# Gated linear attention and a capacity-routed mixture of experts: the low parts of the weights by accumulating DMAs, the middle layer's residuals on GpSimd, and routing operands in other places

## The chip, the cores and the metric

The kernel runs on one core of a Trainium2 chip. The core has a matmul engine (TensorE, PE in the profile), a vector engine (VectorE, DVE), a scalar engine (ScalarE, ACT), GpSimd (POOL), a queue that issues transfers (SyncE, SP), and 16 DMA engines. SBUF is the working memory of 128 partitions; PSUM holds what TensorE writes. The metric is the device time of one execution in microseconds; lower is better.

## The reference

The first part is a linear attention with a decay for each channel, 4 batches of 8 heads, 768 steps, 48 channels. Its output is read as 3072 tokens of 384 values. The second part gives every token to one of 8 experts: the scores are taken in falling order over all tokens and experts, and a token goes to the first expert on its list that has room for it. Each expert takes exactly 384 tokens and applies two layers, 384 to 1024 to 384.

```python
state = alpha[:, :, t, :, None] * state + np.einsum('bhd,bhe->bhde', k[:, :, t], v[:, :, t])
y[:, :, t] = np.einsum('bhd,bhde->bhe', q[:, :, t], state)
...
logits = x @ w_gate
order = np.argsort(-logits.flatten())
for idx in order:
    tok, e = int(idx) // E, int(idx) % E
    if assigned[tok] >= 0 or counts[e] >= cap:
        continue
    assigned[tok] = e
    counts[e] += 1
for e in range(E):
    mask = assigned == e
    h = np.maximum(x[mask] @ w1[e], 0.0)
    out[mask] = h @ w2[e]
```

## The kernel before

The attention stage takes the first 142 us or so. It writes the tokens' rows to a scratch array in HBM (`x_dram`) and leaves the scores of all tokens in SBUF (`L`).

Then two jobs run beside each other to the end.

**Routing.** Experts are filled one after the other, in the order in which they become full. A search (`search`) finds the score at which the next expert has its 384 tokens: the scores' bits are taken as five digits (`BITS`), and for each digit VectorE compares all keys with all values of the digit (`cmp`, L653), TensorE counts by expert with 24 small matmuls (L683), and VectorE decides (`g`, L686), TensorE sums (L690), VectorE takes the digit (`k`, L692) and takes it off the keys (`nd`, L695). At the end of a search some twenty short VectorE instructions find which expert was filled (`es`, `ei`), which tokens it got, and each token's rank in it (`cum`, `rts`, `offs`, `v`). `update` then moves the remaining tokens to their next choice and makes new keys. `extract` turns ranks into row numbers (`idx`, L828), and GpSimd gathers the expert's rows from `x_dram` with three indirect DMAs (`xr`, L833). Many of the small routing operands lie in one PSUM bank (`zb`, "z" in the profile), which the attention no longer needs.

**Experts.** As soon as an expert's number is known, SP loads its weights in two halves, `w1r` and `w2r`, 768 KB each (`weights`). Each matmul operand is used as a rounded high part and a low part, the rest, and each product is taken as high x high, high x low and low x high. `split` makes the parts of the weights: ScalarE copies the high parts `w1h` (L876) and `w2h` (L894). The low part of w2 is made by a ScalarE copy with the sign turned (`w2l`, L892) to which a DMA issued by GpSimd adds the raw weights (L896). The low part of w1 is made by GpSimd, `w1l = w1r - w1h` (L884), in four pieces per half; from the seventh block on each of these pieces waits for the relu of an earlier block (`GATE`, `paced`). `prep` turns the gathered rows with TensorE (L909), copies the high part with ScalarE (`xh`, L914) and subtracts with VectorE (`xl`, L916).

The hidden layer is worked in 8 blocks of 128 units. For a block, `ffn1` does nine matmuls of 128x128 by 128x384 (L930); ScalarE applies the relu (`hf`, L937) and copies the high part (`hh`, L939), VectorE subtracts for the low part (`hl`, L940). `ffn2`, which comes two blocks later, does nine matmuls (L956) into three banks that collect the output over all eight blocks. At an expert's end ScalarE copies the output (`yo`, L961) and GpSimd scatters the rows (L966). PSUM has two banks for the blocks of `ffn1`.

The order in which each engine issues its work is fixed when the kernel is built. `Plan` holds every operation with an engine, an estimated cost, what it reads and writes, and a rank, and simulates the engines: whichever engine can start next takes the operation of the highest rank that is ready. The rank is a base plus the length of the chain behind the operation. The base of routing is 2000 (`CHAIN`), of the extraction 1900 (`SIDE`), and of expert work 1000 less 32 per expert and 3.6 per block (`at`). Each engine then works through its list in order and waits where its next instruction waits. `lat` is the plan's time from a transfer's issue to its landing.

The first expert's second halves of the weights wait until its three gathers have landed (`rows0` and the manual dependency in `weights`).

Of the kernel before, what the change touches and what calls it, by code (L numbers as in the profile page):

```python
# [164 lines left out]
def gla_moe_kernel(ctx, tc, q, k, v, alpha, w_gate, w1, w2, out):  # L165
# [419 lines left out]
    for z in range(2):
        t = {}
        for name, shape, dtype in (
# [3 lines left out]
                ("sg", [NU], I32), ("un", [NU], F32), ("o", [NU, E], BF), ("d0", [NU], BF), ("vi", [NU], I32),  # L591
# [2 lines left out]
        t["nd"] = [rw.tile([128, NU], BF, name=f"nd{z}{j}") for j in range(nb - 1)]
# [68 lines left out]
    def search(i):
# [7 lines left out]
        dh = [("d0", z)] if i else []  # L671
        for t, bits in enumerate(BITS):
# [20 lines left out]
            if not final:  # L693
                nd = s["nd"][t]
                v_(0.24, lambda d=d, nd=nd, t=t: nc.vector.scalar_tensor_tensor(  # L695
                    nd, d, s["k"], dig[:, t + 1], op0=OP.subtract, op1=OP.add),
                   r=H("k") + dh + ["dig"], w=[("nd", z, t)])
# [14 lines left out]
        v_(0.2, lambda: nc.vector.tensor_scalar(s["cl"], ramp, es, None, op0=OP.is_equal), r=H("es"), w=H("cl"))  # L712
# [8 lines left out]
        v_(0.16, lambda: nc.vector.tensor_copy(s["rts"], s["cum"][:, :, NU - 1]), r=[("cum", z, 0), ("cum", z, 1)],  # L721
# [325 lines left out]
```

## Time and profile before

| | |
|---|---|
| median of 3 runs | 479.87 us (474.65 to 480.53) |
| the profiled execution | 480.41 us, span of its instructions 478.7 us |
| attention stage | 0 to about 142 us |
| first matmul of an expert | 179.8 us |
| last row numbers known (`idx`) | 406.6 us |
| last output copied | 469.3 us |

A group's row in the profile names line, engine, operation, output and inputs, the shapes and the count; then the busy time in us, the mean of one in ns, and the idle time of that engine just before these instructions with what ended it. In the list of waits each row names the waiting engine and line, then the one it waited for, the total in us, the number of times and the longest. A row of the timeline begins with the start and the length in us. "Granted clock" is the share of TensorE's full clock that it was given.

### The profile page before, as it was taken

Reading aid. Unit: us, or ns where it says so; the run is one execution under the profiler, and the core shown is the slowest. Engines: PE = TensorE matmul, PEld = TensorE weight load, DVE = VectorE, ACT = ScalarE, POOL = GpSimd, SP = SyncE. Lnnn points to the kernel's source line nnn. Section 1 sums busy time; section 2 is a strip of 40 time slices with the busy share of each in tenths; the row PEclk is TensorE's granted clock in tenths of the full one; section 3 lists DMA queues with packets and bytes.
Section 4 is the critical chain, followed back from the end, with each engine's and each line's share of the span. In section 5 each row is a group of like instructions: output and inputs, shape, how many; then the busy total and the mean of one; then the engine's idle time right before and its main releaser. Section 6 shows DMA issues by size and latency. Waiting matters only on the chain.

```text
span 478.7 us, 11002 instructions
## 1 busy us (share of the span) xinstructions
PE 426.7 (89%) x4326; PEld 379.3 (79%) x4326; DVE 301.6 (63%) x823; ACT 225.2 (47%) x415; POOL 229.2 (48%) x257
## 2 busy tenths in 40 slices
PE   4999999899999778899598889998879989999992
PEld 1788988788887657798498778887769989999991
DVE  6878787978736944955757686775865775222210
ACT  1356555465430035457227447346328557675431
POOL 6767867577500061339126525444228357663402
PEclk9599999999999988799979989999979999999998
DMA  8848987550110057476284484475375199643101
GB/s 295 313 164 276 336 276 224 178 184 18 68 54 16 7 181 195 92 272 149 51 283 98 115 276 105 99 250 148 67 274 151 51 305 370 155 115 67 49 1 51
DMA packets 37684, 76.33 MB, mean 159 GB/s; under 512 B 3584, under 2 KB 17920, under 8 KB 37632
## 3 DMA queue, kind: packets, MB, share of 16 engines
q1 hardware_dynamic: 32256, 53.60, 33.3%
q0 software_dynamic: 5376, 22.02, 19.1%
q8 instruction: 34, 0.56, 0.5%
q14 instruction: 18, 0.15, 0.1%
HBM read 53.59 MB, written 9.44 MB: 132 GB/s over the span
## 4 chain that ended last, share of the span: by engine, by line
PE 64%; DVE 21%; issue 7%; POOL 2%; DMA 2%; ACT 2%; SPq 0%; POOLq 0%; DVEq 0%; ACTq 0%
PE s L930 16%; PE y L956 5%; PE lg L956 5%; PE st L683 5%; PE s L402 5%; PE xt L956 5%; PE xt L390 4%; DVE cmp L653 4%; PE y L453 4%; PE y L446 4%; PE lg L465 2%; DVE te L362 2%; PE s L912 2%; PE st L414 2%; PE xt L909 1%
## 5 line engine op out<-in xcount | busy, mean ns | idle before, releaser
L884 POOL TENSOR_TENSOR w1l<-w1r,w1h 128x384 fp32r<-128x384 f32 x64 | 68.2, 1106 | 57.4 <-ACT hf L937 44.6
L937 ACT ACTIVATE hf<-s 128x384 f32<-128x384 f32 x64 | 31.3, 490 | 101.9 <-PE s L930 73.5
L940 DVE TENSOR_TENSOR hl<-hf,hh 128x384 fp32r<-128x384 f32 x64 | 42.3, 665 | 47.1 <-ACT hh L939 46.9
L833 POOL DMA_INDIRECT xr<-x_dram,idx x24 | 28.5, 1186 | 90.8 <-DVE idx L828 79.7
L930 PE MATMUL s<-xl,w1h 128*128 128x384 f32 x192 | 48.0, 359 | 9.6 <-ACT hf L937 6.4
L930 PE MATMUL s<-xh,w1l 128*128 128x384 f32 x192 | 45.9, 347 | 1.9 <-ACT hf L937 1.9
L966 POOL DMA_INDIRECT out_dram<-yo,idx x24 | 26.9, 1119 | 43.0 <-ACT yo L961 39.4
L930 PE MATMUL s<-xh,w1h 128*128 128x384 f32 x192 | 46.3, 352 | 0.6 <-ACT xh L914 0.6
L930 PEld LDWEIGHTS s<-xl,w1h 128*128 128x128 f32 x192 | 34.2, 196 | 13.5 <-ACT hf L937 9.9
L653 DVE TENSOR_TENSOR cmp<-nd,iota 128x1536 bf16<-128x1536 bf16 (+4 forms) x32 | 41.6, 1310 | 0.8
L876 ACT ACTIVATE w1h<-w1r 128x768 fp32r<-128x768 f32 x32 | 26.0, 834 | 29.6 <-DMA w1r<-in_moe_w_dram 29.6
L683 PEld LDWEIGHTS <-cmp 128*128 128x128 bf16 x816 | 30.4, 118 | 12.1 <-DVE cmp L653 6.9
L372 POOL TENSOR_TENSOR kh<-rk,te 128x512 f32<-128x512 f32 (+1 forms) x24 | 29.4, 1227 | 18.6 <-DVE te L362 14.6
L683 PE MATMUL st<-o,cmp 128*128 128x8 bf16 x816 | 33.1, 175 | 4.8 <-DVE cmp L653 3.8
L402 PE MATMUL s<-qh,kh 64*128 64x128 f32 x384 | 31.6, 301 | 6.2 <-DVE qh L372 5.8
L930 PEld LDWEIGHTS s<-xh,w1l 128*128 128x128 f32 x192 | 34.5, 193 | 2.6 <-issue 1.6
L939 ACT ACTIVATE hh<-hf 128x384 fp32r<-128x384 f32 x64 | 33.6, 526 | 5.6 <-PE y L956 2.6
L405 POOL TENSOR_SCALAR_AFFINE_SELECT sm<-sm 128x1024 f32<-128x1024 f32 x24 | 26.8, 1115 | 18.7 <-ACT sm L404 17.1
L930 PEld LDWEIGHTS s<-xh,w1h 128*128 128x128 f32 x192 | 34.6, 195 | 1.0 <-ACT xh L914 1.0
L402 PEld LDWEIGHTS s<-qh,kh 64*128 64x128 f32 x384 | 25.4, 198 | 11.6 <-DVE qh L372 6.7
L372 POOL TENSOR_TENSOR qh<-rq,tp 128x512 f32<-128x512 f32 (+1 forms) x24 | 29.4, 1227 | 5.2 <-DVE tp L368 4.1
L362 DVE TENSOR_TENSOR_SCAN te<-al,z 128x511 f32<-128x511 f32 (+2 forms) x26 | 30.9, 1189 | 0.9
(193 smaller groups left out, 1019.8 us busy)
## 6 DMA issues: line engine op xcount, KB each, us to landing
w1r<-in_moe_w_dram SPq DMA_DIRECT2D x16, 768.0 KB, 6.1
w2r<-in_moe_w_dram SPq DMA_DIRECT2D x16, 768.0 KB, 8.0
w2l<-w2r POOLq DMA_DIRECT2D x16, 768.0 KB, 6.4
al<-in_alpha_dram SPq DMA_DIRECT2D x24, 260.0 KB, 4.3
rk<-in_k_dram SPq DMA_DIRECT2D x24, 256.0 KB, 4.6
rq<-in_q_dram SPq DMA_DIRECT2D x24, 256.0 KB, 4.1
rv<-in_v_dram SPq DMA_DIRECT2D x24, 192.0 KB, 4.1
x_dram<-xg SPq DMA_DIRECT2D x6, 768.0 KB, 5.3
```

The source lines that it names most:

```text
L362: nc.vector.tensor_tensor_scan(te.t[:, lo:top][:, ::-1], al.t[:, lo + 1:top + 1][:, ::-1], zb[:, lo + 1:top + 1][:, ::-1], al.t[:, 4 * C + ...
L372: eng.tensor_tensor(out_.t[:, us].rearrange("p u c -> p (u c)"), x.t[:, lo:hi], f.t[:, lo:hi], op=OP.mult)
L402: nc.tensor.matmul(sc.t[:, h, u], kh.t[hs, u], qh.t[hs, u], start=True, stop=True)
L653: v_(0.12 + 0.00054 * nt * (js.stop - js.start), lambda js=js: nc.vector.tensor_tensor(words(dst, nt, js), keyed(d, nt, js), each(iotas[t] ...
L683: nc.tensor.matmul(rt[:, 32:40], dst[:, j // U, :, j % U], o[:, j], start=(j == 0), stop=(j == NU - 1))
L833: last_gather[0] = nc.gpsimd.indirect_dma_start(out=xr.t[:, b], out_offset=None, in_=x_dram, in_offset=bass.IndirectOffsetOnAxis(ap=idxs[i ...
L884: x = nc.gpsimd.tensor_sub(l1.t[:, :, c2], r1.t[:, :, c2], h1.t[:, :, c2])
L930: nc.tensor.matmul(o.t.rearrange("p a b -> p (a b)")[:, :CAP], a.t[:, d, cs_], x.t[:, d], start=(n == 0 and d == 0), stop=(n == 2 and d == ...
L937: paced[FB * i + q] = nc.scalar.activation(hf.t, src(), AF.Relu)
L939: add(A_, 0.47, lambda: nc.scalar.activation(hh.t, hf.t, AF.Copy), r=[hf], w=[hh])
L940: v_(0.5, lambda: nc.vector.tensor_sub(hl.t, hf.t, hh.t), r=[hf, hh], w=[hl], port=True)
L956: nc.tensor.matmul(flat(y.t)[:, :Dm], a.t[:, bs], x.t[:, j], start=(q == 0 and n == 0), stop=(q == FB - 1 and n == 2))
```

## The change

- **Low parts of w1.** ScalarE writes `-w1r`, rounded, into `w1l`, in two pieces per half, and a DMA issued by GpSimd adds `w1r` to the whole half, as was done for w2 before. GpSimd's 64 subtractions and their waits for relus (`GATE`, `paced`) are gone. `ffn1`'s third product of each block now needs the sum of the whole half.
- **Residuals of the middle layer.** `hl = hf - hh` moves from VectorE to GpSimd, at a base of 3000, above all other work. VectorE's `xl` also gets a base of 3000.
- **Routing operands.** `rts` is summed by one reduction over `ms` and `qe`, which now lie side by side in PSUM, instead of copied from the ends of the two scans. `ramp` and `pcs` get copies in the PSUM bank for the uses in the chain (`cl`, `oh`). The scaled digits (`dig1`) move from the PSUM bank to SBUF, and the keys (`d0`, `nd`) alternate between two tiles.
- **First expert.** Its second halves of the weights no longer wait for the gathers.
- **The plan's figures.** Landing times of 7.0 us for loads (6.0 before) and 8.5 us for sums (6.0), 0.52 us for `hh`, and 0.035 us between two VectorE operations that follow each other in the PSUM bank (`OWN`).

The diff, without the plan's new bookkeeping of the bank:

```diff
-GATE = 6
-GATHER, LOAD = 3.2, 6.0
+OWN = {"asg", "pen", "dig", "chu", "qe", "m", "ch", "val", "ms", "v1", "ramp"}
+HL_BASE, XL_BASE = 3000.0, 3000.0
+GATHER, LOAD, SUM = 3.2, 7.0, 8.5
...
-    pchu, asg, pm, pch, pqe, pms, pv1 = (mine(120 + NU * j, NU) for j in range(7))
+    pchu, asg, pm, pch, pms, pqe, pv1 = (mine(120 + NU * j, NU) for j in range(7))
+    both = mine(120 + NU * 4, 2 * NU).rearrange("p (a j) -> p a j", j=NU)
...
+    pramp, ppc = mine(296 + NU * E, E), mine(296 + NU * E + E, 1)
+    keys = [rw.tile([128, NU], BF, name=f"key{j}") for j in range(2)]
+    dig1 = rw.tile([128, nb, NU], F32, name="dig1")
...
-                nd = s["nd"][t]
+                nd, kt = keys[(t + 1) % 2], "key%d" % ((t + 1) % 2)
...
-        v_(0.2, lambda: nc.vector.tensor_scalar(s["cl"], ramp, es, None, op0=OP.is_equal), r=H("es"), w=H("cl"))
+        v_(0.2, lambda: nc.vector.tensor_scalar(s["cl"], pramp, es, None, op0=OP.is_equal), r=H("es") + ["ramp"], w=H("cl"))
...
+        def totals():
+            with nc.allow_low_precision(reason="counts up to 24"):
+                nc.vector.tensor_reduce(s["rts"], both, axis=X, op=OP.add)
+        v_(0.2, totals, r=["ms", "qe"], w=H("rts"))
...
-        v_(0.16, lambda: nc.vector.tensor_copy(s["rts"], s["cum"][:, :, NU - 1]), r=[("cum", z, 0), ("cum", z, 1)],
-           w=H("rts"))
...
-            v_(0.28, lambda: nc.vector.scalar_tensor_tensor(pdig, pdi, 1.0, scale, op0=OP.add, op1=OP.mult), w=["dig"])
+            v_(0.28, lambda: nc.vector.scalar_tensor_tensor(dig1, pdi, 1.0, scale, op0=OP.add, op1=OP.mult),
+               r=["dig"], w=["dig1"])
...
-            if i == 0 and hf:
-                tc.add_manual_dep(x.ins, last_gather[0].ins.name, ...
-        wait = ["rows0"] if i == 0 and hf else []
...
+            add(A_, 0.84, lambda c=c: nc.scalar.activation(l1.t[:, :, c], r1.t[:, :, c], AF.Copy, scale=-1.0),
+                r=[r1], w=[(l1, a)])
             add(A_, 0.84, lambda c=c: nc.scalar.activation(h1.t[:, :, c], r1.t[:, :, c], AF.Copy),
                 r=[r1], w=[(h1, a)])
-            for b in range(2):
...
-                    x = nc.gpsimd.tensor_sub(l1.t[:, :, c2], r1.t[:, :, c2], h1.t[:, :, c2])
...
+            if a:
+                add(G_, 1.0, lambda: nc.gpsimd.dma_start(l1.t.bitcast(F32), r1.t, accum_op=OP.add, max_dma_last_dim=8192),
+                    r=[r1, (l1, 0), (l1, 1)], w=[(l1, "sum")], lat=SUM)
...
+            pl.base = XL_BASE
             v_(0.55, lambda x=x, bs=bs: nc.vector.tensor_sub(xl.t[:, :, bs], x.t[:, :DB], xh.t[:, :, bs]),
...
-        for n, (a, x, ra, rx) in enumerate(((h1, xh, (h1, j // 2), xh), (h1, xl, (h1, j // 2), xl), (l1, xh, (l1, j), xh))):
+        for n, (a, x, ra, rx) in enumerate(((h1, xh, (h1, j // 2), xh), (h1, xl, (h1, j // 2), xl), (l1, xh, (l1, "sum"), xh))):
...
-        add(A_, 0.47, lambda: nc.scalar.activation(hh.t, hf.t, AF.Copy), r=[hf], w=[hh])
-        v_(0.5, lambda: nc.vector.tensor_sub(hl.t, hf.t, hh.t), r=[hf, hh], w=[hl], port=True)
+        add(A_, 0.52, lambda: nc.scalar.activation(hh.t, hf.t, AF.Copy), r=[hf], w=[hh])
+        pl.base = HL_BASE
+        add(G_, 1.1, lambda: nc.gpsimd.tensor_sub(hl.t, hf.t, hh.t), r=[hf, hh], w=[hl], port=True)
```

More of the change, by code (lines that the diff above doesn't have):

```diff
@@ L39, in __init__ @@
     def __init__(self):
-        self.ops, self.writer, self.readers, self.base, self.spin = [], {}, {}, 0.0, None
+        self.ops, self.writer, self.readers, self.base, self.spin, self.own = [], {}, {}, 0.0, None, set()
     def buf(self, kind):
@@ L64, in add @@
         before.discard(n)
+        if OWN.intersection(x for x in (*r, *w) if isinstance(x, str)):
+            self.own.add(n)
         self.ops.append((eng, cost, fn, sorted(before), HOP[eng] if lat is None else lat, port, bufs, self.base, mode))
@@ L91, in order @@
         open_ = {i for i in range(n) if not missing[i]}
-        done, ends, last = [], {}, {}
+        done, ends, last, bank = [], {}, {}, {}
         def since(kind, u, eng):
@@ L100, in order @@
                 eng, _, _, _, _, shared, bufs, _, _ = ops[i]
-                t = max(ready[i], free.get(eng, 0.0), port if shared else 0.0)
+                t = max(ready[i], free.get(eng, 0.0), port if shared else 0.0, bank.get(eng, 0.0) if i in self.own else 0.0)
                 for b in bufs:
@@ L116, in order @@
             free[eng] = end - OVER.get(eng, 0.0)
+            bank[eng] = end + SELF.get(eng, 0.0) if i in self.own else 0.0
             if shared:
@@ L590, in gla_moe_kernel @@
                 ("lw", [NU, E], F32), ("offs", [2], F32), ("v", [NU], F32), ("oh", [1], F32), ("sel", [NU], F32),
[L591 removed]
+                ("sg", [NU], I32), ("un", [NU], F32), ("o", [NU, E], BF), ("vi", [NU], I32),
                 ("wi", [NU], I32), ("wb", [NU], BF), ("bk", [NU, NB], F16), ("rhs", [NU, NB], F16), ):
             t[name] = rw.tile([128] + shape, dtype, name=f"{name}{z}")
[L594 removed]
         sets.append(t)
@@ L775, in update @@
         v_(0.35, lambda: nc.vector.tensor_tensor(n["o"], ramp_b, row(chu, E), op=OP.is_equal), r=["chu"], w=[("o", zn)])
-        st.update(chu=chu, o=n["o"], dig=pdig, d=n["d0"], cmp=parts if more else None)
+        st.update(chu=chu, o=n["o"], dig=dig1, d=keys[0], cmp=parts if more else None)
     def search_last(i):
@@ L832, in fetch @@
             def fetch(b=b):
-                last_gather[0] = nc.gpsimd.indirect_dma_start(
+                nc.gpsimd.indirect_dma_start(
                     out=xr.t[:, b], out_offset=None, in_=x_dram,
                     in_offset=bass.IndirectOffsetOnAxis(ap=idxs[i % 4][:, b:b + 1], axis=0))
-            add(G_, 1.2, fetch, r=[("idx", i % 4)] + ([("xd", g) for g in range(NG)] if i == 0 else []), w=[(xr, b)] + (["rows0"] if i == 0 and b == NB - 1 else []), lat=GATHER)
+            add(G_, 1.2, fetch, r=[("idx", i % 4)] + ([("xd", g) for g in range(NG)] if i == 0 else []), w=[(xr, b)], lat=GATHER)
         return xr
@@ L855, in load_w @@
             if which:
-                x = nc.sync.dma_start(r2.t, w2v[bass.ds(ev, 1), :, qs].rearrange("e p c d -> p (e c) d"))
+                nc.sync.dma_start(r2.t, w2v[bass.ds(ev, 1), :, qs].rearrange("e p c d -> p (e c) d"))
             else:
-                x = nc.sync.dma_start(r1.t, w1v[bass.ds(ev, 1), :, :, fs].rearrange("e p c f -> p (e c) f"))
-            if i == 0 and hf:
-                tc.add_manual_dep(x.ins, last_gather[0].ins.name,
-                                  mybir.DependencyInfo(mybir.DependencyClass.Sync, mybir.DependencyReason.DATA),
-                                  reason="rows of the first expert before its later weights")
-        wait = ["rows0"] if i == 0 and hf else []
+                nc.sync.dma_start(r1.t, w1v[bass.ds(ev, 1), :, :, fs].rearrange("e p c f -> p (e c) f"))
         for which, b in ((0, r1), (1, r2)):
-            add("SP", 2.4, lambda which=which: load_w(which), r=[("ei", i % 2)] + wait, w=[b], lat=LOAD)
+            add("SP", 2.4, lambda which=which: load_w(which), r=[("ei", i % 2)], w=[b], lat=LOAD)
         return r1, r2
```

37 lines of the change are left out of this document (12 added, 25 removed).

## The prediction

> **What bounds the kernel now.** I read the page first, then the stretches of 20 us, the groups of TensorE, its waits, and at last the timeline around the longest wait.
>
> ```profile
> span 478.7 us, 11002 instructions
> PE 426.7 (89%) x4326; PEld 379.3 (79%) x4326; DVE 301.6 (63%) x823; ACT 225.2 (47%) x415; POOL 229.2 (48%) x257
> ...
> PE 64%; DVE 21%; issue 7%; POOL 2%; DMA 2%; ACT 2%; SPq 0%; POOLq 0%; DVEq 0%; ACTq 0%
> ```
>
> The chain that ends last is TensorE first, VectorE second; ScalarE, GpSimd and the DMAs hold 2% each. The change touches nothing before 142 us but two small copies, so the expert stage is the one to read. It begins and ends here (timelines of PE and of ACT):
>
> ```profile
> 179.81 2.29 PE L930 MATMUL s<-xh,w1h 128*128 128x384 f32 x6 [0.58 <-ACT xh L914]
> ```
>
> ```profile
> 468.29 0.49 ACT L961 ACTIVATE yo<-y 128x384 f32<-128x384 f32 x1 [2.59 <-PE y L956]
> ```
>
> That is 288.5 us. What must TensorE do in it? The stretches give the pace where nothing disturbs it, and the granted clock where something does (columns: stretch, length, busy us and instructions of PE, PEld, DVE, ACT, POOL, then granted clock, DMA share, GB/s):
>
> ```profile
> 180.00:200.00 20.00, 16.82 (x117) 14.89 (x118) 13.01 (x47) 9.69 (x16) 5.81 (x6) 0.84 0.58 149
> 200.00:220.00 20.00, 20.00 (x183) 18.91 (x183) 12.10 (x28) 11.20 (x19) 8.74 (x8) 0.89 0.73 218
> 240.00:260.00 20.00, 18.74 (x188) 17.36 (x187) 13.78 (x24) 10.22 (x17) 9.31 (x9) 0.87 0.73 225
> 280.00:300.00 20.00, 18.86 (x185) 17.32 (x184) 14.11 (x28) 13.64 (x23) 10.43 (x10) 0.91 0.65 198
> 340.00:360.00 20.00, 15.26 (x118) 13.21 (x119) 14.90 (x54) 4.81 (x10) 5.14 (x6) 0.83 0.70 217
> 440.00:460.00 20.00, 19.42 (x112) 19.10 (x112) 4.46 (x7) 7.35 (x15) 5.76 (x8) 1.00 0.23 59
> ```
>
> In the last row 112 matmuls take 19.42 us, 0.173 us each. The code has 8 experts x 8 blocks x 18 of them, 1152: 199.8 us. To that come the counts of the routing and the turning of rows (groups of PE from 179 us on):
>
> ```profile
> L683 PE MATMUL st<-o,cmp 128*128 128x8 bf16 x648 | 26.1, 176 | 4.0 <-DVE cmp L653 3.8
> L909 PE MATMUL xt<-ident,xr 128*128 128x128 f32 x63 | 10.5, 275 | 0.0
> ```
>
> Together 236.4 us. So 52 us of the stage are not work. The granted clock names a part: 20 us times what is missing in the five rows, 0.16 + 0.11 + 0.13 + 0.09 + 0.17, is 13.2 us. The waits of PE name another (us in total, times, longest):
>
> ```profile
> PE s L930 <- ACT hf L937: 7.1, 12, 0.7
> PE st L683 <- DVE cmp L653: 3.8, 4, 1.8
> PE lg L956 <- DVE hl L940: 3.6, 1, 3.6
> PE s L930 <- DVE xl L916: 3.2, 1, 3.2
> PE st L725 <- DVE rts L721: 2.5, 2, 1.8
> ```
>
> These are 20.2 us, and some 19 us are smaller groups and gaps too short for the view. How the large waits come about is seen around 235 us, on PE and then on DVE:
>
> ```profile
> 234.82 0.42 PE L956 MATMUL lg<-w2h,hh 128*128 128x384 f32 x1
> 238.83 0.69 PE L956 MATMUL lg<-w2h,hl 128*128 128x384 f32 x1 [3.60 <-DVE hl L940]
> ...
> 241.59 0.52 PE L956 MATMUL y<-w2h,hh 128*128 128x384 f32 x1
> 241.91 0.52 PE L956 MATMUL y<-w2h,hl 128*128 128x384 f32 x1
> ```
>
> ```profile
> 229.93 0.23 DVE L701 SCALAR_TENSOR_TENSOR fl<-st,k,ramp 128x8 f32<-128x8 f32 x1
> ...
> 230.41 0.23 DVE L712 TENSOR_SCALAR cl<-ramp,es 128x8 f32<-128x8 f32 x1
> ...
> 237.50 0.16 DVE L773 SCALAR_TENSOR_TENSOR rem<-cl,rem 128x8 f32<-128x8 f32 x1
> ...
> 238.23 0.55 DVE L940 TENSOR_TENSOR hl<-hf,hh 128x384 fp32r<-128x384 f32 x1
> ```
>
> From 229.93 to 238.23 VectorE does nothing but the end of a search and the update of the keys, which the plan ranks over everything. The residual `hl` of a finished middle block waits until its end, TensorE runs dry for 3.60 us, and then its matmuls stand 0.32 us apart (241.59, 241.91) instead of 0.173: a stall and then a stretch at half clock. The wait for `xl` of 3.2 us is the same thing in the row of 340 us.
>
> **The change, part by part.** Rows for the prices:
>
> ```profile
> L884 POOL TENSOR_TENSOR w1l<-w1r,w1h 128x384 fp32r<-128x384 f32 x64 | 68.2, 1106 | 57.4 <-ACT hf L937 44.6 <-ACT w1h L876 9.1 <-issue 3.3
> L896 POOL DMA_DIRECT2D w2l<-w2r x16 | 15.3, 959 | 9.0 <-ACT w2l L892 7.8 <-PE xt L909 1.2
> L892 ACT ACTIVATE w2l<-w2r 128x768 fp32r<-128x768 f32 x32 | 26.7, 834 | 0.1
> L940 DVE TENSOR_TENSOR hl<-hf,hh 128x384 fp32r<-128x384 f32 x64 | 42.3, 665 | 47.1 <-ACT hh L939 46.9
> ```
>
> *Residuals of the middle layer to GpSimd.* VectorE loses 64 x 0.665 = 42.3 us and the 47.1 us that it stood before them. GpSimd does 64 subtractions of the same shape as the `w1l` ones it loses, so 64 x 1.1 us either way. An `hl` takes 0.45 us longer there, and the second layer of a block comes two blocks later (2 x 18 x 0.173 = 6.2 us), which hides relu, copy and subtraction (about 2.1 us). If that cover is gone, 0.45 us x 64 = 29 us would be the cost. The 3.6 us wait goes entirely. Late next is the gather or DMA issue ahead of an `hl` on GpSimd, some 1 us, inside the cover. `xl` stays on VectorE, ranked above the chain: the 3.2 us go, and the chain pays 24 x 0.55 us = 13 us in all, as it does now at other times.
>
> *Low parts of w1 by DMA.* ScalarE gets 32 more scaled copies, 32 x 0.834 = 26.7 us, 3.3 us per expert. It is busy 9 to 14 us of 20 in the rows above, so I cost this at nothing; with no cover it would be 26.7 us. GpSimd issues 16 more DMAs, 15.3 us, and drops the wait for a relu before each subtraction. The transfers:
>
> ```profile
> q0 software_dynamic: 5376, 22.02, 19.1%
> ...
> w1r<-in_moe_w_dram SPq DMA_DIRECT2D x16, 768.0 KB, 6.1
> w2l<-w2r POOLq DMA_DIRECT2D x16, 768.0 KB, 6.4
> ```
>
> The queue took 19.1% of the span, 91 us, for 22.02 MB, of which the 16 sums are 12.6 MB: between 52 us (by bytes) and 91 us (all of it) of the 16 engines for 16 more. The shares of the rows above, 0.58 to 0.73 while routing runs, rise by about 0.2 to 0.3. That is room, but with longer landings. Each half of w1 is now ready only when its whole sum has landed (two copies, an issue of 1 us, 6.4 us), where the first quarter used to need one subtraction. From the third expert on, this is hidden: the fourth's first load is issued at 276.62, its first block done at 310.33 (timelines of SP and ACT).
>
> ```profile
> 276.62 0.38 SPq L858 DMA_DIRECT2D w1r<-in_moe_w_dram  x1
> ```
>
> ```profile
> 310.33 0.49 ACT L937 ACTIVATE hf<-s 128x384 f32<-128x384 f32 x1 [2.60 <-PE s L930]
> ```
>
>  For the first two experts I charge 1 us together, with bounds of 0 and 2 x 6.4 us.
>
> *The first expert's later weights no longer wait for its gathers.* Two loads run beside the gathers: 0 at best, one load's 6.1 us at worst; I take 1.5 us.
>
> *Routing operands.* The totals come straight from `ms` and `qe` in one reduction, skipping a scan and a cast, and `ramp` is read from PSUM:
>
> ```profile
> L721 DVE CAST rts<-cum 128x2 bf16<-128x2 f32 x6 | 2.6, 429 | 0.0
> L712 DVE TENSOR_SCALAR cl<-ramp,es 128x8 f32<-128x8 f32 x6 | 2.4, 400 | 0.0
> L695 DVE SCALAR_TENSOR_TENSOR nd<-nd,k,z 128x24 bf16<-128x24 bf16 x18 | 4.3, 239 | 0.6
> L773 DVE SCALAR_TENSOR_TENSOR rem<-cl,rem 128x8 f32<-128x8 f32 x7 | 2.3, 322 | 0.0
> ```
>
> Tiny operations that average 0.43 and 0.40 us are being held up (`cl` takes 0.23 us at 230.41); about 0.2 us a time should go, 6 x 0.4 us of chain. Of the 2.5 us that PE waits for `rts` I take 2.0 away. But `nd`, which here has one operand in PSUM (`z`) and is never late, gets its digits from SBUF. `rem`, wholly in SBUF, averages 0.322 us for a smaller shape. I cost the move at nothing, since a chain ahead of the experts does not set the end; with no such cover it is the third rival below.
>
> The Trainium skill (SBUF — State Buffer, "Who interferes with whom") says that a VectorE instruction with two SBUF inputs contends with a GpSimd instruction that reads SBUF, and that one with at most one, outside the two-port modes, does not. The trace agrees in `rem` against `nd`; by the rule `nd` gets worse through this edit, and the routing totals better.
>
> *The sum*, against the profiled execution's own 480.4 us (span 478.7 and 1.7 around it; the median of the runs is 479.9): `hl` 3.6, `xl` 3.2, `rts` 2.0, of the waits for `cmp` 1.6 (VectorE is there sooner; GpSimd's subtractions still hold up some), and of the short gaps 2.0. Of the 13.2 us of clock the first row's 3.2 follow the start, which stays; of the other 10 I take 7.5, as three of the four stretches have a wait above before them. The 7.1 us for relu stay. Gains 19.9, costs 2.5: 480.4 - 17.4 = **463 us**.
>
> **The rivals.**
>
> *Everything loosens.* With VectorE apart from the experts, all waits of the list but relu's go (13.1 us), the 10 us of clock, and half of the 19 us: 480.4 - 32.6 = 448 us. For it: the stretch after 400 us, without routing, already runs so. Against: PE keeps one order for two jobs.
>
> *The DMAs eat it.* With both low parts in flight, sums land at 10 us instead of 6.4, and the first block of each expert waits 1.4 us more: 8 x 1.4 = 11 us, 474 us. For it: the DMA shares of 0.73, and gathers share the queue. Against: weights are over 30 us early.
>
> *The placement backfires.* If `nd` meets GpSimd's `hl` as `rem` meets `w1l`, with its excess of 0.16 us over the 0.16 of 237.50, 28 x 0.16 = 4.5 us on a chain that then sets the end: 468 us.
>
> *GpSimd's line.* It works in order, and the experts now depend on it:
>
> ```profile
> POOL xr L833 <- DVE idx L828: 79.7, 5, 36.3
> ```
>
> Its gathers wait for indices, 79.7 us in five waits. Without the first (36.3, before any expert runs), four average 10.9 us. If an `hl` stands behind such a wait, TensorE starves once it exceeds the cover of 6.2 us: 4 x 4.7 us, and 4 half-clock stretches of 3 us, 31 us added to 463: 494 us. Against: the plan ranks `hl` above gathers, and a faster VectorE shortens these waits. It decides if indices come over 6 us later than planned.
>
> **How the numbers follow.** Forecast (456 to 470) 0.42, loosened 0.17, DMAs 0.20, placement 0.07, GpSimd 0.14. The range goes from just under the loosened case, 446, to 486, which leaves out the last rival and the tail of the first. A difference under 2% cannot be told from no change (the three runs differ by 1.2%); 2% below is 470, so faster is 0.42 + 0.17 + 0.07, less 0.04 for forecasts that end above it: 0.62. Same 0.24, slower 0.14.
>
> **What would show it.** Right: `hl` on POOL, DVE about 42 us less busy, no PE wait for it above 1 us, granted clock near 1.00 in the stretches from 220 on. Wrong: PE waits for `w1l` sums or for POOL `hl`; expert blocks no denser than 31 us per expert; POOL waiting for `idx` while `hl` is open.

## The result, and the profile after

The kernel after takes **455.42 us** (median of 3 runs, 455.03 to 461.85) against 479.87: ratio 0.955, with an interval from 0.9415 to 0.9683. The profiled execution took 455.03 us. The gain of 24.5 us is larger than the 17.4 forecast; the time lies inside the range, just under the forecast's own bracket of 456 to 470, between the forecast and the case "everything loosens".

The page of the kernel after, its head and its chain:

```profile
span 453.3 us, 11093 instructions
PE 414.9 (92%) x4351; PEld 370.3 (82%) x4351; DVE 259.8 (57%) x761; ACT 249.2 (55%) x447; POOL 243.9 (54%) x270
...
PE 76%; DVE 11%; DMA 3%; issue 3%; ACT 3%; POOL 1%; SPq 1%; ACTq 0%; POOLq 0%; DVEq 0%
```

VectorE's share of the chain fell from 21% to 11%, and its busy time by 41.8 us. The ends of the expert stage (timelines of PE and ACT):

```profile
177.36 1.30 PE L927 MATMUL s<-xh,w1h 128*128 128x384 f32 x6
```

```profile
442.38 0.50 ACT L956 ACTIVATE yo<-xt 128x384 f32<-128x384 f32 x1
```

That is 265.0 us. The prediction's 288.5 us for before ends at the first of the three last copies; to the last one, at 469.33, it is 289.5. Taking the same 236.4 us of work, 28.6 us are not work, where it was 53.1. The same stretches as before, and one more:

```profile
180.00:200.00 20.00, 18.56 (x170) 16.84 (x169) 14.65 (x53) 9.81 (x18) 7.22 (x7) 1.00 0.91 247
200.00:220.00 20.00, 18.72 (x179) 16.67 (x177) 10.55 (x40) 14.84 (x25) 12.56 (x13) 1.00 0.89 194
240.00:260.00 20.00, 18.72 (x147) 17.02 (x147) 12.66 (x45) 11.10 (x21) 10.52 (x12) 1.00 1.03 225
280.00:300.00 20.00, 18.72 (x148) 17.02 (x147) 15.15 (x54) 9.41 (x18) 9.14 (x11) 1.00 1.03 277
340.00:360.00 20.00, 19.36 (x171) 17.54 (x170) 11.80 (x52) 12.30 (x23) 9.81 (x12) 1.00 0.90 213
360.00:380.00 20.00, 17.14 (x111) 16.49 (x110) 7.36 (x17) 11.66 (x20) 12.50 (x11) 0.91 1.05 350
```

The granted clock is 1.00 in the five rows that lost 13.2 us; the last row, the only one of the stage below it, loses 1.8. The DMA share rose to about 1. TensorE's waits from 160 to 440 us:

```profile
PE s L927 <- ACT hf L932: 8.2, 13, 0.6
PE xt L905 <- DMA xr<-x_dram,idx: 2.9, 1, 2.9
PE st L689 <- DVE cmp L657: 1.2, 4, 0.6
```

The waits for `hl`, `xl` and `rts` are gone. The one new long wait is for gathered rows, in that last row.

Two groups of the kernel after, the moved residual and the keys, which now have both operands in SBUF:

```profile
L935 POOL TENSOR_TENSOR hl<-hf,hh 128x384 fp32r<-128x384 f32 x64 | 72.9, 1139 | 87.8 <-ACT hh L933 47.2
...
L701 DVE SCALAR_TENSOR_TENSOR key<-key,k,dig 128x24 bf16<-128x24 bf16 x24 | 7.9, 328 | 0.7
```

### The profile page after: what moved, and what is told of

It is laid out like the page before. It is cut to its first block, busy times and chain, and to the rows that moved or that the text cites. A ratio compares the mean times of both kernels' runs of the same rounds, so it can differ in the third digit from the quotient of the medians.

```text
span 453.3 us, 11093 instructions
## 1 busy us (share of the span) xinstructions
PE 414.9 (92%) x4351; PEld 370.3 (82%) x4351; DVE 259.8 (57%) x761; ACT 249.2 (55%) x447; POOL 243.9 (54%) x270
## 4 chain that ended last, share of the span: by engine, by line
PE 76%; DVE 11%; DMA 3%; issue 3%; ACT 3%; POOL 1%; SPq 1%; ACTq 0%; POOLq 0%; DVEq 0%
PE s L927 23%; PE xt L951 7%; PE y L951 7%; PE lg L951 7%; PE st L689 6%; PE s L406 4%; PE y L457 4%; PE y L450 4%; PE xt L394 4%; PE s L908 3%; DMA al<-in_alpha_dram 2%; PE lg L469 2%; PE xt L905 2%; DVE cmp L657 2%; DVE te L366 2%
## 5 line engine op out<-in xcount | busy, mean ns | idle before, releaser
L935 POOL TENSOR_TENSOR hl<-hf,hh 128x384 fp32r<-128x384 f32 x64 | 72.9, 1139 | 87.8 <-ACT hh L933 47.2
L927 PE MATMUL s<-xl,w1h 128*128 128x384 f32 x192 | 46.2, 349 | 5.7 <-ACT hf L932 5.7
L927 PE MATMUL s<-xh,w1h 128*128 128x384 f32 x192 | 44.8, 344 | 0.6 <-ACT hf L932 0.6
L657 DVE TENSOR_TENSOR cmp<-key,iota 128x1536 bf16<-128x1536 bf16 (+4 forms) x38 | 44.4, 1178 | 0.9
L927 PEld LDWEIGHTS s<-xl,w1h 128*128 128x128 f32 x192 | 33.0, 189 | 8.6 <-ACT hf L932 8.6
L892 POOL DMA_DIRECT2D w2l<-w2r x16 | 16.1, 1008 | 42.6 <-DVE g L692 31.8
L888 ACT ACTIVATE w2l<-w2r 128x768 fp32r<-128x768 f32 x32 | 26.7, 833 | 22.3 <-DVE sel L758 22.2
L409 POOL TENSOR_SCALAR_AFFINE_SELECT sm<-sm 128x1024 f32<-128x1024 f32 x24 | 26.8, 1117 | 18.0 <-ACT sm L408 16.4
L927 PEld LDWEIGHTS s<-xh,w1l 128*128 128x128 f32 x192 | 33.9, 190 | 3.0 <-ACT hf L932 2.9
L406 PEld LDWEIGHTS s<-qh,kh 64*128 64x128 f32 x384 | 25.0, 195 | 11.7 <-DVE qh L376 6.5
L913 DVE TENSOR_TENSOR xl<-xt,xh 128x384 fp32r<-128x384 f32 x23 | 12.6, 552 | 35.2 <-ACT xh L910 35.1
L460 ACT ACTIVATE yt<-y 128x512 f32<-128x512 f32 x24 | 14.3, 598 | 32.1 <-PE y L457 32.0
L961 POOL DMA_INDIRECT out_dram<-yo,idx x24 | 24.3, 1015 | 14.0 <-ACT yo L956 11.3
## 6 DMA issues: line engine op xcount, KB each, us to landing
w2r<-in_moe_w_dram SPq DMA_DIRECT2D x16, 768.0 KB, 10.5
```

The lines of the kernel that those rows point to most:

```text
L406: nc.tensor.matmul(sc.t[:, h, u], kh.t[hs, u], qh.t[hs, u], start=True, stop=True)
L409: add(G_, 1.15, lambda: nc.gpsimd.affine_select(sm.t, sm.t, pattern=[[0, 8], [1, C]], compare_op=OP.is_ge, fill=0.0, base=0, channel_multi ...
L657: v_(0.12 + 0.00054 * nt * (js.stop - js.start), lambda js=js: nc.vector.tensor_tensor(words(dst, nt, js), keyed(d, nt, js), each(iotas[t] ...
L888: add(A_, 0.84, lambda q2=q2: nc.scalar.activation(l2.t[:, q2], r2.t[:, q2], AF.Copy, scale=-1.0), r=[r2], w=[(l2, a)])
L927: nc.tensor.matmul(o.t.rearrange("p a b -> p (a b)")[:, :CAP], a.t[:, d, cs_], x.t[:, d], start=(n == 0 and d == 0), stop=(n == 2 and d == ...
L935: add(G_, 1.1, lambda: nc.gpsimd.tensor_sub(hl.t, hf.t, hh.t), r=[hf, hh], w=[hl], port=True)
```

## The experiments

All ratios are to the kernel before on the same chip. "First" and "last" are the first and the last relu of the expert stage, from the timelines of ScalarE in the profiled execution; between them lie the 64 blocks, so their distance is the **pace**, and "first" carries the **start**. "Gap" is the 0.035 us of the plan between two operations in the PSUM bank. A pace comes from one execution, and the times of one kernel spread (474.7 to 481.6 us for the kernel before, on the chip of e1), so a few us between two paces tell nothing.

| kernel | w1l by | hl on | gap | ratio (95%) | first, last | pace |
|---|---|---|---|---|---|---|
| before | GpSimd | VectorE | no | 1 | 185.2, 464.6 | 279.4 |
| after | DMA | GpSimd | yes | 0.955 (0.9415 to 0.9683) | 182.8, 437.0 | 254.2 |
| e1 | DMA | VectorE | yes | 0.9454 (0.9379 to 0.953) | 184.3, 435.9 | 251.6 |
| e2, before with ranks | GpSimd | VectorE | no | 0.9849 (0.9763 to 0.9934) | 183.9, 452.1 | 268.2 |
| e3, e2 with hl moved | GpSimd | GpSimd | no | 0.9757 (0.9672 to 0.9842) | 184.7, 451.6 | 266.9 |
| e4, placement undone | DMA | GpSimd | yes | 0.9654 (0.9566 to 0.9741) | 183.8, 442.2 | 258.4 |
| e5 | DMA | VectorE | no | 0.981 (0.9774 to 0.9845) | 195.4, 456.7 | 261.3 |
| e6 | GpSimd | VectorE | yes | 1.0493 (1.0445 to 1.0541) | 192.3, 491.9 | 299.6 |
| e7 | GpSimd | GpSimd | yes | 1.0868 (1.0804 to 1.0933) | 191.0, 506.2 | 315.2 |
| e8, no sums for w1l | none | GpSimd | yes | 0.9382 (0.9364 to 0.94) | 183.6, 439.2 | 255.6 |
| e9, e6 with digits in PSUM | GpSimd | VectorE | yes | 1.0028 (0.9985 to 1.0072) | 185.1, 463.5 | 278.4 |
| e10, digits in PSUM | DMA | GpSimd | yes | 0.9451 (0.9395 to 0.9508) | 183.0, 437.0 | 254.0 |
| e11, e1 with other banks | DMA | VectorE | yes | 0.9239 (0.9175 to 0.9303) | 182.7, 427.7 | 245.0 |
| e12 | DMA | GpSimd | no | 0.9761 (0.9696 to 0.9825) | 194.7, 459.1 | 264.4 |

**e1: is it the engine of `hl`?** The kernel after, with `hl` back on VectorE at the experts' rank:

```diff
-        pl.base = HL_BASE
-        add(G_, 1.1, lambda: nc.gpsimd.tensor_sub(hl.t, hf.t, hh.t), r=[hf, hh], w=[hl], port=True)
+        v_(0.5, lambda: nc.vector.tensor_sub(hl.t, hf.t, hh.t), r=[hf, hh], w=[hl], port=True)
```

> The kernel after, with one part undone: the middle layer's residual hl is subtracted by VectorE again, at the experts' rank below the routing chain; the low parts of w1 stay with the DMAs, so GpSimd has no subtraction at all. Engine theory (the gain came from taking hl out of VectorE's line): the stalls at the end of each search come back, PE waits of about 3 us for hl or relu and half-clock stretches in the 20 us windows, 455 + 7 (waits) + 8 (clock) = about 470 us; 465 to 476. DMA theory (the gain came from freeing GpSimd of the subtractions that hold up VectorE's short instructions): those are gone entirely here, so it stays at 455 or falls to 452.

453.25 us, no slower than after. TensorE's waits from 160 us on, and the group of `hl`, in e1:

```profile
PE s L927 <- ACT hf L932: 8.1, 14, 0.6
PE st L689 <- DVE cmp L657: 1.7, 4, 0.8
```

```profile
L934 DVE TENSOR_TENSOR hl<-hf,hh 128x384 fp32r<-128x384 f32 x64 | 35.5, 555 | 52.3 <-ACT hh L933 52.0
```

No wait for `hl`, though it has neither the other engine nor the high rank, and a piece takes 0.555 us where it took 0.665. The time is the one that the second theory above gave, and the mechanism that the prediction put first is not needed for the gain.

**e2 and e3: the ranks, and `hl` on GpSimd, on the kernel before.** e2 gives `xl` and `hl` the base 3000 and leaves them on VectorE; e3 also moves `hl`:

```diff
+            pl.base = 3000.0
             v_(0.55, lambda x=x, bs=bs: nc.vector.tensor_sub(xl.t[:, :, bs], ...
...
+        pl.base = 3000.0
-        v_(0.5, lambda: nc.vector.tensor_sub(hl.t, hf.t, hh.t), ...            # stays in e2
+        add(G_, 1.1, lambda: nc.gpsimd.tensor_sub(hl.t, hf.t, hh.t), ...       # in e3
```

> The kernel before with one thing added: hl and xl, both still on VectorE, are ranked above the routing chain in the plan (base 3000). Rank theory (the stalls came from the plan's order on VectorE, and the rank alone cures them): waits of PE for hl and xl vanish, granted clock near 1.00, about 480 - 6.8 - 8 = 465 us or lower. Engine theory: the 64 subtractions now lengthen the chain in its update by 3 or 4 times 0.55 us and it has to wait for ScalarE's copies in order, so a part of the gain only, 470 to 476 us; w1l's pacing stays.

> The kernel before with hl moved to GpSimd and hl and xl ranked at 3000; GpSimd keeps the 64 paced subtractions for w1l, so it has 128 subtractions, and the routing operands stay where they were. Engine theory: hl out of VectorE is what counts; the stalls go, but GpSimd has 2 x 68 us of subtractions and the short VectorE instructions meet it twice as often: 458 to 468 us. DMA theory (the low parts of w1 by DMA are needed, as GpSimd cannot carry both): PE waits for w1l or hl on POOL, 472 us or more.

471.3 and 467.92 us. Both times lie in the ranges of the engine theory, but the waits do not bear it out: in e2 none for `hl` or `xl` is left, with `hl` still on VectorE. The ranks alone give 8.6 us by the medians (11.2 us of pace, in the fastest of e2's four executions); moving the engine adds 3.4 us (1.3 us of pace), and the intervals overlap. So on the kernel before the ranks remove these waits, and what the engine adds is within the noise.

**e4: the placement.** The kernel after with `ramp` and `pcs` read from SBUF, the digits in PSUM and `rts` copied from the ends of the scans:

```diff
-                nc.vector.tensor_reduce(s["rts"], both, axis=X, op=OP.add)
+        v_(0.16, lambda: nc.vector.tensor_copy(s["rts"], s["cum"][:, :, NU - 1]), ...
-        ... nc.vector.tensor_scalar(s["cl"], pramp, es, ...
+        ... nc.vector.tensor_scalar(s["cl"], ramp, es, ...
-    dig1 = rw.tile([128, nb, NU], F32, name="dig1")
+    dig1 = mine(0, 120).rearrange("p (t j) -> p t j", j=NU)
```

> The kernel after, with the routing operands put back: ramp and pcs read from SBUF, the digits in the PSUM bank, rts cast from the ends of the scans. Engine theory: TensorE is the bound and routing runs ahead, so at most 1 to 2 us slower, 455 to 458 us; key below 0.25 us mean, rts and cl above 0.3 us. Placement theory (a good part of the gain comes from the shorter end of a search): PE waits for rts of 2 us or more come back, 460 us or more.

461.63 us, some 6 us more than after, without the waits for `rts` that the placement theory expected. The groups of VectorE, TensorE's wait for the comparisons, and one comparison and GpSimd at the same time, in e4:

```profile
L657 DVE TENSOR_TENSOR cmp<-key,iota 128x1536 bf16<-128x1536 bf16 x12 | 16.0, 1336 | 0.4
...
L716 DVE TENSOR_SCALAR cl<-ramp,es 128x8 f32<-128x8 f32 x6 | 1.3, 224 | 0.0
...
L726 DVE CAST rts<-cum 128x2 bf16<-128x2 f32 x7 | 1.2, 172 | 0.2
```

```profile
PE st L687 <- DVE cmp L657: 4.5, 6, 1.5
```

```profile
312.57 2.07 DVE L657 TENSOR_TENSOR cmp<-key,iota 128x1536 bf16<-128x1536 bf16 x1
```

```profile
312.80 1.02 POOL L931 TENSOR_TENSOR hl<-hf,hh 128x384 fp32r<-128x384 f32 x1
```

`cl` and `rts` take 0.224 and 0.172 us in their old places, so they are not what costs. The comparisons of 128x1536 take 1.336 us each where e1 has 0.958 (its row stands below, and after has the same mean), and the wait for them is 4.5 us instead of 1.2. Twelve of them by 0.38 us are 4.5 us, most of the loss. From 177 us on four of them take 2.07 to 2.18 us, and during each of these GpSimd does one `hl`; the seven others take 0.96 us and meet none, and in the kernel after none of them meets one. That the changed order of the lists brings them together is argued, not shown.

**e5 and e12: the plan's gap.** e1, and the kernel after, without the new bookkeeping of the bank:

```diff
-OWN = {"asg", "pen", "dig", "chu", "qe", "m", "ch", "val", "ms", "v1", "ramp"}
+OWN = set()
```

> As e1 (the kernel after with hl on VectorE), and the plan no longer knows of the gap between VectorE operations in the PSUM bank (OWN is empty); nothing else changes in the operations. Theory of the late hl, with the gap as the reason that e1 has no stall (the plan lets an hl in wherever a chain operation would have to wait 0.035 us): blocks whose hl ends more than 4 us after its copy return, up to 8 or 12 us, PE waits for hl, 462 to 472 us. Theory of GpSimd's subtractions (the gain came from GpSimd having no subtraction for w1l): no change, 452 to 455 us.

> The kernel after, hl on GpSimd, and the plan no longer knows of the gap between VectorE operations in the PSUM bank (OWN empty, as in e5). If the gap matters only as the door by which an hl on VectorE gets into the update of the keys (e1 453, e5 474): with hl on GpSimd no change, 453 to 458 us. If the plan needs it for a good order of the chain in any case: 464 us or more.

474.26 and 476.51 us: ratios of 0.981 and 0.976. Most of the gain is gone on either engine: the second case of e12, and outside both ranges of e5. In e5 `hl` ends up to 8.5 us behind its `hh` again (3.5 in e1), but TensorE has no wait for it, and e12 loses as much with at most 3.0 us. The start shows a first reason. VectorE's timeline of the kernel after, then of e12, where the first expert's number `ei` is written:

```profile
156.22 0.17 DVE L727 SCALAR_TENSOR_TENSOR z<-cl,z 128x8 f32<-128x8 f32 x1
156.31 0.15 DVE L712 TENSOR_SCALAR ei<-es 128x1 int32<-128x1 f32 x1
```

```profile
164.07 0.14 DVE L712 TENSOR_SCALAR ei<-es 128x1 int32<-128x1 f32 x1
```

In the plan an operation in the bank (z) cannot start until 0.035 us after another one there, so the list first takes one from outside, whatever its rank: `ei` slips in 7.8 us earlier. The loads of w1 hang on it, then their sums (timelines of SP and of POOL, after and then e12):

```profile
158.41 0.96 SPq L867 DMA_DIRECT2D w1r<-in_moe_w_dram  x2
```

```profile
173.55 2.00 POOL L885 DMA_DIRECT2D w1l<-w1r  x2
```

```profile
166.17 2.00 SPq L867 DMA_DIRECT2D w1r<-in_moe_w_dram  x2
```

```profile
183.32 0.89 POOL L885 DMA_DIRECT2D w1l<-w1r  x1 [2.21 <-ACT w1l L880]
```

And so TensorE's list in e12:

```profile
177.68 0.87 PE L905 MATMUL xt<-ident,xr 128*128 128x128 f32 x3 [3.73 <-issue]
...
186.25 0.77 PE L927 MATMUL s<-xl,w1h 128*128 128x384 f32 x3
186.95 0.18 PE L696 MATMUL st<-g,one 64*128 64x8 bf16 x1
190.25 0.16 PE L733 MATMUL st<-rts,tri 128*128 128x2 bf16 x1 [3.12 <-DVE rts L725]
...
191.94 0.60 PE L756 MATMUL st<-cs,oh 65*128 65x8 f32 x2 [1.50 <-DVE oh L754]
192.39 2.27 PE L927 MATMUL s<-xh,w1l 128*128 128x384 f32 x6
```

The first gathered rows are turned at 177.68, after a wait of 3.73 us; the kernel before turns them at 174.56, the kernel after at 174.17. From 174 to 176 us, inside this wait, the DMA share is 1.07 in e12 and 0.39 in before: four loads have been issued from 165.56 on, where the kernel before issues two ahead of its gathers. That the loads make the rows late is read from this, not tested. The first product with `w1l` comes at 192.39 instead of 181.14 (the same view of the kernel after), and from 186.95 until then TensorE has no expert work between its routing matmuls: the idle time shows as a wait for `rts`, of 3.12 us. Just before its own matmul for `rts` the kernel after runs nine second-layer matmuls. The stretch of e12:

```profile
180.00:200.00 20.00, 12.75 (x107) 11.17 (x106) 15.55 (x56) 12.26 (x19) 5.53 (x6) 0.59 0.87 172
```

The clock falls to 0.59 here. The first block is done 11.9 us later than after, and the pace loses 10.2 us more; in e5 against e1 it is 11.1 and 9.7. The loss of pace can be read from waits and clock between the first and the last relu: TensorE's listed waits are 16.8 us in e12 and 11.7 in after, and at clocks of 0.97 and 0.99 some 7.9 and 2.5 us are missing, together 10.5 us more. In e5 and e1 it is 15.1 and 10.4 us of waits and 5.2 and 0 us of clock, 9.9 us more. In e12 most of the lost clock is the end of the start's half-clock stretch (0.83 from 200 to 220), and the largest new wait is for `o`, the last operation of an update (4.7 us).

**e6 and e9: both engine moves undone.** The kernel after with `w1l` subtracted by GpSimd, paced as before, and `hl` on VectorE; e9 also puts the digits back into PSUM:

```diff
-            add(A_, 0.84, lambda c=c: nc.scalar.activation(l1.t[:, :, c], r1.t[:, :, c], AF.Copy, scale=-1.0), ...
-            if a:
-                add(G_, 1.0, lambda: nc.gpsimd.dma_start(l1.t.bitcast(F32), r1.t, accum_op=OP.add, ...
+            for b in range(2):
+                add(G_, 1.2, sub, r=[r1, (h1, a)] + ([("pace", n)] if n >= 0 else []), w=[(l1, 2 * a + b)], port=True)
...
-    dig1 = rw.tile([128, nb, NU], F32, name="dig1")                            # in e9 only
+    dig1 = mine(0, 120).rearrange("p (t j) -> p t j", j=NU)
```

> The kernel after with both engine moves undone: hl on VectorE, w1l by paced subtractions on GpSimd, as before; what stays of the change is the placement of routing operands, the rank of xl, the gap in the plan and the earlier loads of the first expert. Theory of the late hl: no hl is late, as in e1, so most of the gain stays, 455 to 460 us. Theory of GpSimd's subtractions: the gain of e1 is lost, 465 us or more, with VectorE's short instructions held up (rts, wi, cmp means up).

> As e6 (both engine moves undone, the rest of the change kept, 507 us against 484 of before), and the scaled digits go back to the PSUM bank. In e6 the 27 key instructions, which read two SBUF operands, took 25.5 us in all instead of 6.5, up to 4.27 us each, behind GpSimd's bursts of four subtractions. If that is what makes e6 slow: key back at 0.24 us, PE's wait for cmp (22.8 us in e6) below 6 us, 472 to 486 us against the same before. If the plan's new figures or the lost pacing order are the cause: 500 us or more still.

507.46 us (5% slower than before) and 481.86 us (no difference). The keys in e6, as a group, and the longest one on the timelines of VectorE and GpSimd; then the keys in e9:

```profile
L702 DVE SCALAR_TENSOR_TENSOR key<-key,k,dig 128x24 bf16<-128x24 bf16 x24 | 24.7, 1030 | 0.6
```

```profile
394.09 4.27 DVE L702 SCALAR_TENSOR_TENSOR key<-key,k,dig 128x24 bf16<-128x24 bf16 x1
```

```profile
394.00 3.88 POOL L889 TENSOR_TENSOR w1l<-w1r,w1h 128x384 fp32r<-128x384 f32 x4
```

```profile
L702 DVE SCALAR_TENSOR_TENSOR key<-key,k,z 128x24 bf16<-128x24 bf16 x24 | 5.7, 238 | 0.6
```

The key begins with a row of four subtractions and ends 0.48 us after the last of them. With its digits in PSUM the same operation takes 0.238 us, and TensorE's wait for `cmp` is 7.5 us (its row stands below) where e6 has 22.8. That placement costs e6 some 22 us (0.0465 of 480, by the two ratios).

e9 differs from e1 in the making of `w1l` and the digits' place. Both have the ranks of `xl`, the gap and the totals. In e9, groups of VectorE and waits of PE; then e1's group of comparisons:

```profile
L946 DVE TENSOR_TENSOR hl<-hf,hh 128x384 fp32r<-128x384 f32 x64 | 47.4, 741 | 44.1 <-ACT hh L945 43.4
...
L658 DVE TENSOR_TENSOR cmp<-key,iota 128x1536 bf16<-128x1536 bf16 x12 | 18.2, 1518 | 0.3
```

```profile
PE st L690 <- DVE cmp L658: 7.5, 6, 3.9
PE xt L914 <- DVE xl L922: 3.7, 4, 1.2
```

```profile
L657 DVE TENSOR_TENSOR cmp<-key,iota 128x1536 bf16<-128x1536 bf16 x12 | 11.5, 958 | 0.4
```

Without GpSimd's subtractions of w1, `hl` takes 0.555 us instead of 0.741 and these comparisons 0.958 instead of 1.518; TensorE's waits for `cmp` and `xl` shrink from 11.2 to 1.7 us, and the pace from 278.4 to 251.6. Between the first and the last relu all listed waits are 25.3 us in e9 and 10.4 in e1, and at clocks of 0.95 and 1.00 some 14 us and none are missing: together about 29 us, which covers the 26.8. The number of GpSimd's subtractions is not what counts: the kernel after has 64 as well, `hl` in place of `w1l`, and its comparisons of 128x1536 average 0.958 us like those of e1.

**e7: only `w1l` back on GpSimd.** As e6, with `hl` left on GpSimd.

> The kernel after with only the low parts of w1 undone: paced subtractions on GpSimd again, hl stays on GpSimd, so 128 subtractions. Theory of the late hl: as after, 455 to 459 us. Theory of GpSimd's subtractions: e3's 468 less the 6 us that the placement gave in e4, 460 to 464 us, with more idle of PE at the experts' starts.

523.41 us. TensorE's longest waits in e7:

```profile
PE xt L914 <- DVE xl L922: 14.9, 8, 4.6
PE st L690 <- DVE cmp L658: 12.5, 6, 5.5
PE xt L914 <- DMA xr<-x_dram,idx: 11.9, 3, 6.4
```

This is far above both ranges. With both kinds of subtraction on GpSimd and the digits in SBUF, TensorE's waits for `xl`, `cmp` and the gathered rows are 39.3 us. Against e6, the engine of `hl` costs 16 us here. Against after, which differs only in how `w1l` is made, the pace loses 61.0 us: with `hl` on GpSimd and the digits in SBUF the sums are worth more than twice what e9 against e1 shows.

**e8: are the adding DMAs hidden?** The kernel after without the 16 sums for w1:

```diff
-            if a:
-                add(G_, 1.0, lambda: nc.gpsimd.dma_start(l1.t.bitcast(F32), r1.t, accum_op=OP.add, max_dma_last_dim=8192), ...
```

> The kernel after without the 16 DMAs that add w1r: w1l stays the negated copy, so the third product of the first layer is left wrong; it measures what these transfers cost. If they are hidden (weights come over 30 us early): 453 to 457 us. If they lengthen the gathers, as the one wait for xr of 2.9 us and its stretch at 0.91 clock suggest: 449 to 452 us.

453.38 us, with a pace of 255.6 against 254.2 with the sums. Its transfers, then those of the kernel after (columns: size, median us to landing):

```profile
w1r<-in_moe_w_dram SPq DMA_DIRECT2D x16, 768.0 KB, 5.8
w2l<-w2r POOLq DMA_DIRECT2D x16, 768.0 KB, 5.9
```

```profile
w1r<-in_moe_w_dram SPq DMA_DIRECT2D x16, 768.0 KB, 9.0
w2l<-w2r POOLq DMA_DIRECT2D x16, 768.0 KB, 8.5
w1l<-w1r POOLq DMA_DIRECT2D x16, 768.0 KB, 6.8
```

With the sums the loads of w1 land 3.2 us later and the sums of w2 2.6 us. The time is 2 us above that of e8; by the ratios, each on its own chip, it is some 3 us (0.9382 here, 0.9451 in e10), and the intervals just touch. So the sums are hidden but for a few us at most.

**e10: only the digits back in PSUM.**

```diff
-    dig1 = rw.tile([128, nb, NU], F32, name="dig1")
+    dig1 = mine(0, 120).rearrange("p (t j) -> p t j", j=NU)
```

> The kernel after with one piece of the placement undone: the scaled digits are read from the PSUM bank again; the totals by one reduction and the copies of ramp and pcs stay. In the kernel after, the key instructions lose 2.3 us in all to GpSimd. If SBUF is the worse place for the digits: 453 to 455 us. If the 6 us that e4 lost came from the digits (operations in one bank follow each other with a gap, and the plan orders by it): 458 to 462 us. If they came from the totals and ramp: no change, 455 us.

454.94 us, as after. Here, where GpSimd has no bursts of subtractions for `w1l`, the digits' place does not matter. By elimination the 6 us of e4 belong to the totals and the copies of `ramp` and `pcs`; no run undid these alone.

**e11: what are the waits for the relu?** In both kernels 7 to 8 us of TensorE's waits are for `hf`, 0.6 us each, at the starts of experts. The two PSUM buffers of the hidden layer were two halves of one tile (`s`). e11 is e1 with two tiles:

```diff
...
-    HB = Kind([SC.tiles[0][:, h] for h in range(2)])
-    YF = [Kind([x]) for x in (YB.tiles[0], LG.tiles[0], XT.tiles[1])]
+    HB = Kind([YB.tiles[0], XT.tiles[1]])
+    YF = [Kind([x]) for x in (SC.tiles[0][:, 0], SC.tiles[0][:, 1], LG.tiles[0])]
...
```

> As e1 (hl on VectorE, 453 us), and the two PSUM buffers of the hidden layer lie in two tiles (y and xt) instead of two halves of one tile (s); the three output buffers take s and lg. In e1 PE waits 8.1 us for relu, 14 times 0.58 us, at experts' starts, where the relu of one block begins only after a product into the other half of the tile, and the next product into that half waits for this relu. If that is a dependency by tile and not by need: PE's waits for relu fall below 2 us, 445 to 450 us. If the two banks themselves are the limit (a block's buffer is free only after its relu): no change, 452 to 455 us.

445.56 us, ratio 0.9239 (0.9175 to 0.9303): faster than both kernels. TensorE's waits in e11:

```profile
PE s L950 <- ACT yo L955: 2.3, 4, 0.6
PE xt L905 <- DMA xr<-x_dram,idx: 2.2, 3, 1.0
```

No wait for the relu is left. They were a dependency between two halves of one tile, which no data needed; now the outputs in the halves of `s` have a smaller one (2.3 us).

## Why the prediction was right, and where it was wrong

**What bounds the kernel: right.** TensorE's 236 us of work stayed; the idle time and the half-clock stretches behind it shrank from 53.1 to 28.6 us. Of these 24.5 us, 11.4 are clock, 7.9 are the listed waits (20.2 against 8.2 + 2.9 + 1.2), and 5.2 are smaller groups and short gaps, for which the prediction took 2.0. `hl` went to GpSimd, VectorE lost 41.8 us of busy time, and no wait for `hl` remained, as listed under "what would show it". One sign of being wrong came true by its number, a pace above 31 us per expert (254.2 us for 63 steps are 32.3 per 8), but the sign was set wrong: the forecast itself implies 271 us for eight experts, 33.9 each.

**The step that failed is the cause.** "Residuals of the middle layer to GpSimd" was to remove the waits. The waits of 3.6 and 3.2 us did go, but e1 loses them with `hl` on VectorE. In three pairs the engine changes the pace by 1.3 (e2, e3), 2.6 (e1, after) and 3.1 us (e5, e12), in both directions; in a fourth (e6, e7) GpSimd is 15.6 us worse. I read a wait for `hl` behind a chain on VectorE as a matter of the engine; it was in part one of rank (e2) and for the most part of what held VectorE up (e9 against e1). That the time came into the range is in part luck: the sum counted the waits that would go, and another part of the change than the one it named removes them.

**Low parts of w1 by DMA: the mis-sized term.** I charged 1 us and foresaw no gain. It has two sides. In the pace it gives 26.8 us with the gap (e9 against e1; the digits' place, the other difference, is without effect in e10), 61.0 with `hl` on GpSimd and the digits in SBUF (e7 against after), and at most 18.1 without the gap (before against e5, which also has the new placement and the rank of `xl`). The rows of `hl`, `cmp` and the keys show GpSimd's subtractions holding up VectorE. I had named that as 1.6 us of waits for `cmp` that the subtractions in part cause, though the groups of before held the price (0.400 us for a `cl` that takes 0.23 undisturbed). At the start the kernels with the sums lose 10 us where `ei` is as late as before (185.2 against 195.4 and 194.7), which is inside the bound of 2 x 6.4 that I gave and did not take. Not all of it is the sums: in e12 the first product comes 2.5 us later than in before (182.34 against 179.81), behind the late gathers, and the first product with `w1l` 8.7 us later (192.39 against 183.72). No run separates the sums from the loads beside the gathers.

**A part I gave no line of the sum: the plan's gap.** It pays that start back: `ei` comes 7.8 us earlier, and the first block is done at 182.8. I read the plan's new figures as bookkeeping. Without the DMAs, the gap, the totals and the rank of `xl` together gain nothing (e9, 1.0028); the DMAs without the gap give 2% (e5, e12), both 4.5 to 5.5% (after, e1). The other 10 us of pace that go with the gap are waits for routing and clock, by the figures of e12 and e5 above; which shift in the lists brings these waits was not followed up.

**Placement.** Forecast 2.0 us, through `cl` and `rts`; measured about 6, and not through those: through comparisons that meet GpSimd's `hl` (e4).

**Clock.** Forecast 7.5 us, measured 13.2 - 1.8 = 11.4. The first stretch's 3.2 us, which I took to belong to the start and to stay, went too. In rows of 2 us some 2.0 of them lie from 180 to 184 (clocks of 0.50 and 0.52), behind a wait for gathered rows that is 0.3 us in the kernel after; the other 1.2 lie from 196 on (0.89 and 0.50), behind a wait for `rts`, which is gone. Both in the kernel before:

```profile
178.33 0.90 PE L909 MATMUL y<-ident,xr 128*128 128x128 f32 x3 [1.60 <-DMA xr<-x_dram,idx]
...
196.20 0.16 PE L725 MATMUL st<-rts,tri 128*128 128x2 bf16 x1 [1.81 <-DVE rts L721]
```

**Costs.** ScalarE's 26.7 us of copies were hidden, as said: no wait of TensorE for them is listed in the kernel after. The 1.5 us for loads beside gathers did not come, since with `ei` early the loads are issued 10 us before the gathers; with `ei` late, in e12, TensorE stands 3.73 us there. The relus' waits stayed, as said; e11 shows that they need not.

**The rivals.** "Everything loosens" came as near as the forecast: of the listed waits of before only the relu's is left above 1.2 us, and 11.4 of the clock's 13.2 us went, 1.4 more than it said. "The DMAs eat it" happened at most once, the 2.9 us and 1.8 us of clock at 375 us, under a DMA share of 1.05; that the sums cause it is not shown, as at this place e8, without them, waits 1.2 us and e1, with them, 1.0. "GpSimd's line" did not: by the timelines of ScalarE and GpSimd, `hl` ends at most 3.07 us after its `hh`, inside the cover of 6.2. "The placement backfires" is real as a mechanism and small here: 24 keys by 0.09 us, 2.2 us (0.328 against 0.238), without effect on the time (e10). With GpSimd subtracting in bursts it is some 22 us (e6 against e9). The Trainium skill (SBUF — State Buffer, "Who interferes with whom") states that conflict for two SBUF inputs; the keys agree with it, by their time with one operand in PSUM.

**Open.** The low parts by DMA on the kernel before with nothing else changed, e11 with `hl` on GpSimd, and e11's banks on the kernel after were not tried. Nor were the first expert's earlier loads and the plan's other new figures undone alone. Why the engine of `hl` costs 16 us in e7 was not separated from the digits in SBUF. In the plan GpSimd's subtractions, the comparisons and `hl` exclude one another (`port`), so taking `w1l` off GpSimd also changes the order of the lists; how much of the gain is that, and how much the shorter instructions, no run separates.

## What to carry to other kernels

A wait names the operation that came last, not the reason why it was late: before the engine is changed, try the rank, and look at what lengthens that engine's instructions beyond their undisturbed time. An edit that makes an operand later at the start (a sum instead of a first piece) has to be weighed with the time at which its chain begins, down to the one small instruction that releases the loads. Where the order is planned, a new figure in the plan is an edit of the kernel, and two buffers that are halves of one tile may wait for each other.

## What the runs showed of the hardware

- A VectorE instruction of 0.24 us with both operands in SBUF waited through four GpSimd subtractions in a row, not through one: 4.27 us, ending 0.48 us behind the fourth (e6). A comparison of 0.96 us during which GpSimd does one subtraction of 1.02 us takes 2.07 us (e4).
- With the 16 adding DMAs the DMA shares of the stretches shown are 0.89 to 1.05, and the loads of w1 land in 9.0 us instead of 5.8; the kernel without them is faster by 2 to 3 us, at the edge of the noise (e8).
- In e12 the granted clock, in rows of 2 us, is 0.50 from 176 to 186, during and behind the wait of 3.73 us, and again from 190 to 206, during and behind waits of 3.12, 1.50 and 1.97 us. From 180 to 200 that is 0.59: 20 x 0.41 = 8.2 us of full clock are missing. A shorter wait was followed by it too: in before, after 1.81 us, 0.50 from 198 to 204.
